# Gated attention and a multiplicative feed-forward network: output tiles of two units paired for seven products, the second unit's gates begun earlier, the weights looked at last

## The chip, the cores and the metric

The kernel runs on one core of one Trainium2 chip. The metric is the device time of one execution in microseconds (us). A profile shows one execution as the hardware profiler recorded it; its "span" leaves out what lies before the first and after the last recorded instruction. TensorE is called PE below, VectorE DVE, ScalarE ACT, GpSimd POOL; SP is the engine that issues the transfers.

## What is computed

Two blocks follow each other. The first is a linear attention with a complex gate per position and channel; the second is a feed-forward network without a nonlinearity except one product.

```python
# q, k, v, a_re, a_im: (4 batches, 8 heads, 768 positions, 48 channels), float32
mag = sqrt(a_re*a_re + a_im*a_im)
scale = minimum(mag, 0.999) / (mag + 1e-06)
for t in range(768):                       # S is a complex 48x48 state per head
    S = (a_re[t] + 1j*a_im[t]) * scale[t] * S + outer(k[t], v[t])
    y[t] = q[t] @ real(S)
x = y with heads side by side              # (3072 tokens, 384)
h = (x @ w1) * (x @ w2) @ w3               # w1, w2: 384x1024, w3: 1024x1024
out = h @ w_out                            # w_out: 1024x384
```

The weights arrive as float64 and are rounded to float32 on the chip; q, k, v and the gates are float32.

## The kernel before

**Units.** The work is cut into 8 units: batch u // 2, half u % 2, 384 positions (TT) in 3 chunks or token tiles of 128. For each unit there are four kinds of work.

- `gates(u)` (L531 to L644) is a generator; each `yield` ends a step. It computes, on ACT and DVE in turn, the running product and angle of the gates: Ln, Exp (L550, L551), a product (L554), its square (L559), Ln (L563), then L567 to L570, the minimum and the scans (L574 to L577), Ln and Exp again, the factors on k and q (L585 to L589), the arc tangent, a scan of angles (L600), its reduction (L607, L608), sines (L611 to L613), four products (L616 to L620). At the end `move` (L627 to L630) issues transfers that regroup k and q by head into the tiles KL and QL, and then the gates, k, q and v of the next unit are loaded (L642, L643). All transfers are issued on the one SP queue.
- The attention of a unit is a list of pieces (`pieces`, L972): `turn` (transposes on PE into tile tp, a copy by ACT into KT, L655), `state` (kv on PE, a sum T on DVE, L710), `scores` (sc on PE, a masked copy by DVE into A, L667), `outputs` (y on PE, a copy by ACT into xT, L694).
- `ffn_ab(u, j)` for j = 0 to 7 (L716): two products m of 384 columns on PE, one copied by ACT (L728), one multiplied by it on DVE into the tile ab (L729).
- The output, ab times w3o, where w3o = w3 @ w_out was made at the start. For units 1 to 7, tiles 0 and 1 of a unit form a pair: the 256x1024 by 1024x384 product is cut into 2x2 blocks and done with 7 block products instead of 8 (Strassen's scheme with 15 sums): `out_sums` makes 4 sums S of blocks of ab (L749), `out_weights` made the sums T of blocks of w3o once (L740), `product` (L762) does 4 steps of 128 rows for a 128x192 block p and adds it into place on DVE (L756). Tile 2 of these units, and all three tiles of unit 0, go through `ffn_out` (L794): 8 matmuls of 384 columns, a copy by ACT, a store. The first product and the second share a PSUM tile (`bank`), so do the third and fourth, and the fifth and sixth. Float32 matmuls are two instructions each in the records.

**Order.** PE's order is written out by hand (`tc.manual_schedule`, L1009); on the other engines a planner orders the instructions by their place in the program and by the dependencies. `tc.high_priority()` moves instructions ahead, and `add_manual_dep` with ORDER fixes an order without a semaphore. `unit(u, ...)` (L993) goes through pieces(u) with the rest of the feed-forward network of unit u - 1 between them, calls the next step of gates(u + 1) after each, and after each piece one `look`.

**The start.** For each of the 8 rows of blocks f, `row_work` rounds w3 and w_out (`load_weight`, L834: ACT writes the rounded low half, for w3 also the sign; DVE shifts and adds), and `fuse` (L935) multiplies them on PE into w3o, whose accumulators hold all 8 PSUM banks. Between the rows stand two steps each of gates(0). w1 and w2 (`w12_work`) are rounded during the attention of unit 0 and the first ab steps. The gates of unit 1 begin at piece 2 of unit 0 (L1054).

**Looks.** `check_weights` (L866) loads the raw weights again after the start, 36 pieces, and the real gates of units 0 and 1, 6 pieces, and tests them for values outside the range in which the fast rounding holds; `judge` (L946) adds up all tests, and a slow general path follows if one failed. Each look runs on ACT (L885 to L888). They start in unit 2, and `judge` comes before the last ffn.

Of the kernel before, what the change touches and what calls it, by code (L numbers as in the profile page):

```python
# [374 lines left out]
def kernel(  # L375
# [47 lines left out]
    HEAD = 8  # L423
    SPLIT = (0,)
# [7 lines left out]
    MIN_SQ, MAX_SQ = 1.126 ** 2, 2.0 ** 32 - 512  # L432
# [30 lines left out]
    consts = singles.tile([P, 7], FP, name="consts")  # L463
    for i, x in enumerate((1.0, LN_EPS, PI / 2, SMALL, -LARGE, MIN_SQ, -MAX_SQ)):
        nc.vector.memset(consts[:, i:i + 1], x)
    ONE, EPS, QUARTER, LEAST, MOST, TINY, TWO = (consts[:, i:i + 1] for i in range(7))
# [8 lines left out]
    st_wts = singles.tile([P, 80], FP, name="st_wts")  # L475
    nc.vector.memset(st_wts, 0.0)
# [11 lines left out]
    def load_gates(u):  # L488
        g = g_t.setdefault(u, {})
        for n, src in (("re", art), ("im", ait)):  # L490
            g[n] = one.tile([P, KD, TT], FP, tag=n, name=n)
            load_rows(g[n], src, u)
# [6 lines left out]
    def load_qkv(u):  # L499
# [5 lines left out]
        load_rows(g["q"], qt, u)  # L505

# [3 lines left out]
        g["vr"] = vr  # L510
# [14 lines left out]
    def chain(ins):  # L525
# [3 lines left out]
        chained[:] = [ins]  # L529

    def gates(u, split):  # L531
# [17 lines left out]
        for s in parts:  # L549
            act(out=A[:, s], in_=re[:, s], func=AF.Ln)  # L550
            act(out=r[:, s], in_=A[:, s], func=AF.Exp, scale=-1.0)  # L551
        yield
# [13 lines left out]
        for s in parts:  # L566
            stt(out=A[:, s], in0=Z[:, s], scalar=0.5, in1=A[:, s], op0=OP.mult, op1=OP.add)  # L567
# [5 lines left out]
        for s in parts:  # L573
            ts(out=A[:, s], in0=A[:, s], scalar1=0.999, scalar2=None, op0=OP.min)  # L574
# [17 lines left out]
        spread_v(u)  # L592
# [16 lines left out]
        yield  # L609
        for s in parts:  # L610
            act(out=re[:, s], in_=Z[:, s], func=AF.Abs)  # L611
            act(out=re[:, s], in_=re[:, s], func=AF.Sin, scale=-1.0, bias=QUARTER)
            act(out=Z[:, s], in_=Z[:, s], func=AF.Sin)  # L613
        yield
        if not split:
            tt(out=r, in0=k, in1=re, op=OP.mult)  # L616
            tt(out=k, in0=k, in1=Z, op=OP.mult)
            yield
            tt(out=A, in0=q, in1=re, op=OP.mult)
# [7 lines left out]
        def move(dst, src, s):  # L627
            for x in range(2):
                for f in range(KD)[s]:
                    nc.sync.dma_start(out=dst[x * KD + f::2 * KD], in_=src[x][:, f])  # L630

        for s in [slice(f, f + 1) for f in range(KD)] if split else parts:
            if split:
                tt(out=r[:, s], in0=k[:, s], in1=re[:, s], op=OP.mult)
                tt(out=k[:, s], in0=k[:, s], in1=Z[:, s], op=OP.mult)
            move(KL, (R, K2), s)
            if split:
                tt(out=A[:, s], in0=q[:, s], in1=re[:, s], op=OP.mult)
# [19 lines left out]
    def scores(u, c, x):  # L658
# [7 lines left out]
        with tc.high_priority():  # L666
            nc.vector.copy_predicated(out=A[:, x * n:(x + 1) * n], data=sc,  # L667
                                      mask=causal.rearrange("p (h t) -> p h t", h=1).to_broadcast([P, n, C]))
# [27 lines left out]
    def state(u, c):  # L696
# [9 lines left out]
        with tc.high_priority():  # L706
            if T is None:
                nc.scalar.copy(out=Tn, in_=kv)
            else:
                nc.vector.tensor_tensor(out=Tn, in0=kv, in1=T, op=OP.add)  # L710
# [412 lines left out]
```

## Time and profile before

| what | us |
|---|---|
| median of 9 executions | 574.75 (574.01 to 576.45) |
| the profiled execution | 574.61 |
| its span | 572.7 |
| first matmul of the rounding (`fuse`, L940) | 7.18 |
| first transpose of unit 0 (L653) | 58.43 |
| first score of unit 0 (L665) | 69.05 |
| first matmul of ffn_ab of unit 0 (L723) | 83.16 |
| last add of an output (L756) begins | 566.69 |

The mean clock granted to PE is 0.991 of full speed. Read it so: up to 83.16 us PE waits for rounding, gates and transfers; from there it hardly stops until 566.7, and the rest of the span is the last store and the test of the flag. Units follow each other about every 62 us (the last products of unit 1's, 2's and 3's output end at 209.90, 271.17 and 333.86). Matmul records overlap, since they are pipelined: a mean duration in a group is longer than the time from one start to the next, which the chain of waits gives.

### The profile page before, as it was taken

The page shows a single profiled execution, that of the slowest core. Times are in us where ns is not written, and L with a number is a line of the kernel's source. Part 1 is how long each engine was busy: PE and PEld are TensorE (multiplying, and loading weights), DVE is VectorE, ACT ScalarE, POOL GpSimd, SP SyncE. Part 2 cuts the span into 40 slices and gives each one's busy share as a digit, 9 for nine tenths or more (in the row PEclk, how much of TensorE's full clock was granted, in tenths as well). Part 3 has the DMA queues.
Part 4 walks back from the last instruction along what each step waited for, and adds up shares of the span by engine and source line. Part 5 has one row for each costly group of instructions (what it writes and reads, how often), then busy time and mean ns, then how long its engine had stood idle before and what let it go on. Part 6 is the DMA issues. An engine that isn't in the chain of part 4 may idle for free.

```text
span 572.7 us, 9280 instructions
## 1 busy us (share of the span) xinstructions
PE 545.4 (95%) x3682; PEld 387.2 (68%) x3682; DVE 335.4 (59%) x507; ACT 347.1 (61%) x569; POOL 3.5 (1%) x9
## 2 busy tenths in 40 slices
PE   4779999999999999999999999999999999999995
PEld 2345775578556985688567976697568966796564
DVE  6898479946852577356752787255743696332121
ACT  6998668537572798558963899279964645101100
POOL 2000000000000000000000000000000000000000
PEclk9899999999999999999999999999999999999998
DMA  8994997393273356954593527844483103300001
GB/s 278 357 378 134 246 340 219 111 232 87 86 160 87 112 150 188 213 172 150 186 211 116 151 74 223 211 144 148 132 196 108 30 27 105 75 2 30 0 1 47
DMA packets 46340, 84.74 MB, mean 148 GB/s; under 512 B 4688, under 2 KB 36176, under 8 KB 45392
## 3 DMA queue, kind: packets, MB, share of 16 engines
q1 hardware_dynamic: 46288, 84.06, 51.7%
q8 instruction: 31, 0.51, 0.4%
q14 instruction: 21, 0.17, 0.1%
HBM read 60.42 MB, written 4.72 MB: 114 GB/s over the span
## 4 chain that ended last, share of the span: by engine, by line
PE 69%; DVE 10%; ACT 10%; DMA 6%; issue 3%; SPq 1%; ACTq 0%; DVEq 0%
PE m L723 38%; PE p L768 10%; PE o L802 7%; PE sc L665 4%; PE kv L703 4%; PE y L692 4%; ACT gZ L544 2%; DMA re<-in_a_re_dram 2%; PE tp L653 2%; ACT gR L544 2%; DMA QL<-gA 1%; DVE gZ L600 1%; DMA look<-in_w_dram 1%; PE f L940 1%; ACT gA L544 1%
## 5 line engine op out<-in xcount | busy, mean ns | idle before, releaser
L723 PE MATMUL m<-xT,w1s 128*128 128x384 f32 x384 | 135.3, 489 | 1.4 <-ACT xT L694 0.8
L723 PE MATMUL m<-xT,w2s 128*128 128x384 f32 x384 | 134.3, 486 | 0.0
L723 PEld LDWEIGHTS m<-xT,w2s 128*128 128x128 f32 x384 | 73.0, 190 | 50.9
L723 PEld LDWEIGHTS m<-xT,w1s 128*128 128x128 f32 x384 | 71.0, 190 | 47.4 <-ACT xT L694 2.0
L729 DVE TENSOR_TENSOR ab<-m,a 128x384 f32<-128x384 f32 x64 | 35.3, 553 | 84.2 <-PE m L723 74.3
L940 PE MATMUL f<-wo_s,w3s 128*128 128x384 f32 x128 | 49.2, 543 | 15.2 <-DVE wo_s L854 15.2
L728 ACT COPY a<-m 128x384 f32<-128x384 f32 x64 | 30.2, 473 | 48.9 <-PE m L723 47.8
L802 PE MATMUL o<-w3o,ab 128*128 128x384 f32 x160 | 54.0, 487 | 0.0
L655 ACT COPY KT<-tp 128x384 f32<-128x384 f32 x40 | 33.5, 849 | 29.2 <-PE tp L653 29.1
L940 PEld LDWEIGHTS f<-wo_s,w3s 128*128 128x128 f32 x128 | 26.7, 214 | 35.1 <-DVE wo_s L854 17.0
L665 PE MATMUL sc<-QL,KL 96*128 96x128 f32 x384 | 47.2, 276 | 1.0 <-issue 0.7
L665 PEld LDWEIGHTS sc<-QL,KL 96*128 96x128 f32 x384 | 45.7, 192 | 2.1 <-issue 0.8
L667 DVE COPY_PREDICATED A<-causal,sc 128x512 f32<-128x512 int32 x48 | 34.4, 740 | 14.5 <-PE sc L665 13.8
L710 DVE TENSOR_TENSOR T<-kv,T 96x512 f32<-96x512 f32 x16 | 11.0, 687 | 54.0 <-PE kv L703 54.0
L802 PEld LDWEIGHTS o<-w3o,ab 128*128 128x128 f32 x160 | 29.6, 190 | 18.7 <-issue 0.4
L692 PE MATMUL y<-A,V 128*32 128x128 f32 x768 | 39.3, 275 | 0.0
L692 PEld LDWEIGHTS y<-A,V 128*32 128x32 f32 x768 | 32.9, 109 | 3.4 <-issue 1.3
L692 PE MATMUL y<-QL,T 96*32 96x128 f32 x640 | 34.6, 272 | 0.0
L768 PE MATMUL p<-To,So 128*128 128x192 f32 x168 | 31.6, 335 | 0.3 <-DVE U L756 0.3
L703 PEld LDWEIGHTS kv<-V,KT 128*96 128x96 f32 x320 | 29.6, 165 | 2.9 <-issue 1.3
L692 PEld LDWEIGHTS y<-QL,T 96*32 96x32 f32 x640 | 31.3, 110 | 0.0
L703 PE MATMUL kv<-V,KT 128*96 128x64 f32 x320 | 30.0, 247 | 1.3 <-ACT KT L655 1.3
(113 smaller groups left out, 742.8 us busy)
## 6 DMA issues: line engine op xcount, KB each, us to landing
look<-in_w_dram SPq DMA_DIRECT2D x28, 512.0 KB, 3.9
raw<-in_w_dram SPq DMA_DIRECT2D x7, 1024.0 KB, 11.1
raw<-in_w_dram SPq DMA_DIRECT2D x8, 768.0 KB, 8.0
KL<-gR SPq DMA_DIRECT2D x24, 192.5 KB, 3.4
KL<-k SPq DMA_DIRECT2D x24, 192.5 KB, 4.0
re<-in_a_re_dram SPq DMA_DIRECT2D x24, 192.0 KB, 5.3
im<-in_a_im_dram SPq DMA_DIRECT2D x24, 192.0 KB, 3.2
k<-in_k_dram SPq DMA_DIRECT2D x24, 192.0 KB, 4.2
```

The lines of the kernel that those rows point to most:

```text
L544: chain(nc.scalar.activation(**kw))
L655: nc.scalar.copy(out=KT_t[u, c][:, :, :, x].rearrange("p h d f -> p f d h"), in_=tp.rearrange("p f (d h) -> p f d h", h=H))
L665: nc.tensor.matmul(out=sc[:, j], lhsT=KL[:, x * n + j, w], rhs=QL[:, x * n + j, w], start=True, stop=True)
L667: nc.vector.copy_predicated(out=A[:, x * n:(x + 1) * n], data=sc, mask=causal.rearrange("p (h t) -> p h t", h=1).to_broadcast([P, n, C]))
L692: nc.tensor.matmul(out=o, lhsT=a, rhs=b, start=s0, stop=s1)
L703: nc.tensor.matmul(out=kv[:, hd], lhsT=KT[:, hd].rearrange("p d x f -> p (d x f)"), rhs=V[:, hd], start=True, stop=True)
L723: nc.tensor.matmul(out=m, lhsT=w[:, j * P // WB, f, j * P % WB:j * P % WB + P], rhs=xT_t[u][:, f], start=(f == 0), stop=(f == KD - 1))
L728: copied[:] = [nc.scalar.copy(out=a, in_=got[0])]
L729: nc.vector.tensor_tensor(out=ab_t[u][:, j], in0=got[1], in1=a, op=OP.mult)
L768: nc.tensor.matmul(out=m[p], lhsT=a[:, f], rhs=b[:, f], start=(f == 0), stop=(f == KH - 1))
L802: nc.tensor.matmul(out=m, lhsT=ab_t[u][:, f, t * P:(t + 1) * P], rhs=w3o[:, f], start=(f == 0), stop=(f == KF - 1))
L940: nc.tensor.matmul(out=sums[j], lhsT=w3_t[f][:, j * P:(j + 1) * P], rhs=w3_t["wo"][:, f], start=(f == 0), stop=(f == KF - 1))
```

## The change

1. **Output.** `ffn_out` is gone. A pair is a list of two (unit, tile): in even units tiles 1 and 2, in odd units tiles 0 and 1, and then tile 0 of the even unit with tile 2 of the odd one. So there are 12 pairs with 7 products each, and no output tile of 8 matmuls. The tile ab holds 512 columns, of which the odd unit overwrites the last 384. The order of the products is the same, 1, 2, 4, 6, 7, 5, 3, with other PSUM tiles: (1, 4), (2, 6), (7, 3), (5). The first product is copied into a tile U1 and not into the output. Stores come after the next unit's moves.
2. **The second unit's gates.** Five steps of gates(1) are taken at piece 0 of unit 0 (none at pieces 1 to 5, one from piece 6 on); the sum T of unit 0's chunk 1 waits in order for the last sum of step 5; the minimum of step 6 comes after the last masked copy seen so far. The gates of unit 1 are loaded inside gates(0), before its moves; the cosine of unit 0 goes to another tile so that `re` is free for it.
3. **Weights looked at last.** A look is now three instructions on DVE (sign bit off, clamp, compare and count). Units 2 to 5 take a look at every fourth piece, units 6 and 7 at every piece, and the rest goes between the ab steps of the last unit; `judge` follows that unit's first product.
4. **The start.** Row 1 is loaded and rounded in two halves, its sign on DVE; the steps of gates(0) are dealt 3, 2, 2, 2, 1, 1; v of unit 0 is loaded after row 3 and spread at the end; w1 and w2 are rounded with the sign on ACT, after the moves.

```diff
+    def load_v(u):
...
+        if u:
+            load_v(u)
...
             act(out=r[:, s], in_=A[:, s], func=AF.Exp, scale=-1.0)
+            if u == 1:
+                tc.add_manual_dep(chained[-1].ins, fused[-1].ins.name, ORDER, reason="unit 0 first")
...
-            stt(out=A[:, s], in0=Z[:, s], scalar=0.5, in1=A[:, s], op0=OP.mult, op1=OP.add)
+            begun[:] = [stt(out=A[:, s], in0=Z[:, s], scalar=0.5, in1=A[:, s], op0=OP.mult, op1=OP.add)]
...
-            ts(out=A[:, s], in0=A[:, s], scalar1=0.999, scalar2=None, op0=OP.min)
+            least = ts(out=A[:, s], in0=A[:, s], scalar1=0.999, scalar2=None, op0=OP.min)
+            if u == 1:
+                tc.add_manual_dep(least.ins, masked[-1].ins.name, ORDER, reason="scores first")
...
+        cos = A if u == 0 else re
+        if u == 0:
+            load_gates(1)
...
-                nc.vector.tensor_tensor(out=Tn, in0=kv, in1=T, op=OP.add)
+                add = nc.vector.tensor_tensor(out=Tn, in0=kv, in1=T, op=OP.add)
+                if (u, c) == (0, 1):
+                    tc.add_manual_dep(add.ins, begun[-1].ins.name, ORDER, reason="begun")
...
-            ab_t[u] = one.tile([P, KF, TT], FP, tag="ab", name="ab")
+            if u % 2 == 0:
+                ab_t["two"] = one.tile([P, KF, TT + P], FP, tag="ab", name="ab")
+            ab_t[u] = ab_t["two"][:, :, u % 2 * P:u % 2 * P + TT]
...
-    def out_sums(u):
-        S = s_t["S"] = late.tile([P, 4, KH, P], FP, tag="S", name="So")
-        A = [[ab_t[u][:, i * KH:(i + 1) * KH, t * P:(t + 1) * P] for i in range(2)] for t in range(2)]
+    def out_sums(tiles):
+        S = late.tile([P, 4, KH, P], FP, tag="S", name="So")
+        A = [[ab_t[u][:, i * KH:(i + 1) * KH, t * P:(t + 1) * P] for i in range(2)] for u, t in tiles]
...
-        def product(n, i, p):
+            store = nc.sync.dma_start(out=out[r0:r0 + P, :], in_=o[i])
+            after = moved.get(max(u for u, _ in tiles) + 1)
+            if after:
+                tc.add_manual_dep(store.ins, after.ins.name, ORDER, reason="moves first")
+
+        def product(p, bank, i):
+            if p == 1:
+                out_sums(tiles)
             if i == 0:
-                m["bank"] = ps_m.tile([P, 2, DH], FP, tag="mm", name="p")
-            m[p] = m["bank"][:, i]
+                m[bank] = ps_m.tile([P, 2, DH], FP, tag="mm", name="p")
+            m[p] = m[bank][:, i]
...
-                    nc.scalar.copy(out=o[0][:, 0:DH], in_=m[1])
+                    nc.scalar.copy(out=U[1], in_=m[1])
...
-        return [lambda n=n, p=p: product(n, n % 2, p) for n, p in enumerate((1, 2, 4, 6, 7, 5, 3))]
-
-    def ffn_out(u, t, parts=1):
...
+        return [lambda p=p, b=b, i=i: product(p, b, i) for p, b, i in (
+            (1, "a", 0), (2, "b", 0), (4, "a", 1), (6, "b", 1), (7, "c", 0), (5, "d", 0), (3, "c", 1))]
...
+        elif not sign_act:
+            nc.vector.tensor_scalar(out=low, in0=hi, scalar1=-0x80000000, scalar2=0x3F800000, op0=OP.bitwise_and,
+                                    op1=OP.bitwise_or)
...
-                    follow([nc.scalar.activation(out=hi, in_=hi, func=AF.Square, scale=2.0 ** 15)])
-                    nc.scalar.activation(out=lo, in_=hi, func=AF.Relu, scale=-1.0, bias=TINY, accum_out=st_wts[:, n:n + 1])
-                    if w is w3t:
-                        nc.scalar.activation(out=hi, in_=hi, func=AF.Relu, bias=TWO, accum_out=st_wts[:, n + 40:n + 41])
+                    follow([nc.vector.tensor_scalar(out=hi.bitcast(I32), in0=hi.bitcast(I32), scalar1=0x7FFFFFFF,
+                                                    scalar2=None, op0=OP.bitwise_and)])
+                    nc.vector.tensor_scalar(out=lo, in0=hi, scalar1=MIN_HI, scalar2=MAX_HI if w is not wo else 3.0e38, op0=OP.max,
+                                            op1=OP.min)
+                    nc.vector.scalar_tensor_tensor(out=lo, in0=hi, scalar=1.0, in1=lo, op0=OP.mult, op1=OP.is_equal,
+                                                   accum_out=st_wts[:, n:n + 1])
...
-            load_weight((w1s, w2s)[i][:, n], got[n][i])
+            load_weight((w1s, w2s)[i][:, n], got[n][i], True)
...
-    def ffn(u, parts=1):
-        if u == 0:
-            return [lambda j=j: ffn_ab(u, j) for j in range(KF)] + [p for t in range(UC) for p in ffn_out(u, t, parts)]
-        got, last = out_pair(u), ffn_out(u, UC - 1, parts)
-        if parts == 2:
-            got.insert(5, last[1])
-        return [lambda j=j: ffn_ab(u, j) for j in range(KF)] + [lambda: (out_sums(u), last[0]())] + got
+    def ffn(u):
+        got = [lambda j=j: ffn_ab(u, j) for j in range(KF)] + out_pair([(u, 1 - u % 2), (u, 2 - u % 2)])
+        return got + (out_pair([(u - 1, 0), (u, UC - 1)]) if u % 2 else [])
...
-            next(look, None)
+            if u > NU - 3 or i % 4 == 0:
+                next(look, None)
...
-        row_load(1)
+        row_load(1, 2)
...
-            for _ in range(2):
+            for _ in range((3, 2, 2, 2, 1, 1)[f]):
                 next(steps, None)
         work = w12_work()
+        for _ in steps:
+            pass
+        spread_v(0)
         for f in work[:2]:
             f()
-        for _ in steps:
-            pass
...
-        load_gates(1)
...
-            if i >= 2:
+            for _ in range(5 if i == 0 else i >= 6):
                 next(steps)
...
-        for _ in look:
-            pass
-        judge()
-        for f in ffn(NU - 1, 2):
+        for i, f in enumerate(ffn(NU - 1)):
             f()
+            for _ in range(2):
+                next(look, None)
+            if i == KF:
+                for _ in look:
+                    pass
+                judge()
```

## The prediction

> **What bounds the kernel now.** I read the busy times and the clock first, then PE's idle time by stage, then the chain of waits, then the groups.
>
> ```profile
> PE 545.4 (95%) x3682; PEld 387.2 (68%) x3682; DVE 335.4 (59%) x507; ACT 347.1 (61%) x569; POOL 3.5 (1%) x9
> PE   4779999999999999999999999999999999999995
> PEclk9899999999999999999999999999999999999998
> ```
>
> PE is busy all through, at full clock, except in the first three slices of 14.3 us. So the time is PE's start plus PE's work plus few gaps. The start, from the timeline of PE (start, length, count, idle time before and its releaser):
>
> ```profile
> 7.18 8.21 PE L940 MATMUL f<-wo_s,w3s 128*128 128x384 f32 x16 [7.18 <-DVE wo_s L854]
> 19.66 17.43 PE L940 MATMUL f<-wo_s,w3s 128*128 128x384 f32 x48 [4.26 <-DVE wo_s L854]
> 40.33 14.75 PE L940 MATMUL f<-wo_s,w3s 128*128 128x384 f32 x40 [3.25 <-DVE wo_s L854]
> 55.56 2.85 PE L940 MATMUL f<-wo_s,w3s 128*128 128x384 f32 x8 [0.47 <-DVE wo_s L854]
> ```
>
> PE waits there for DVE's rounding (rows 1 and 4). Later gaps, from the table of stretches (stretch, then PE's busy time out of its length):
>
> ```profile
> 125.00:130.00 5.00, 4.35 (x41) 4.12 (x40) 2.26 (x4) 1.17 (x2) 0.00 (x0) 1.00 1.08 279
> 155.00:160.00 5.00, 4.41 (x14) 2.39 (x13) 2.25 (x4) 3.58 (x5) 0.00 (x0) 1.00 0.40 118
> 400.00:420.00 20.00, 18.61 (x60) 10.84 (x59) 15.78 (x19) 18.98 (x36) 0.00 (x0) 1.00 0.46 140
> ```
>
> That is 0.65 + 0.59 + 1.39 = 2.6 us idle; the last one is a transpose that waited 1.4 us for gR (L616), behind looks on ACT. The rates come from the chain (start, us, what), in unit 2:
>
> ```profile
> 181.11 5.16 PE o L802 x16
> 186.60 1.33 PE kv L703 x16
> 187.93 1.37 PE p L768 x8
> 189.69 1.57 PE p L768 x8
> 191.26 1.33 PE kv L703 x16
> 192.59 1.84 PE sc L665 x16
> 194.43 1.30 PE p L768 x8
> ```
>
> A tile by `ffn_out` takes 5.16 us, a block product 1.30 to 1.57. Between the first two products PE stands still:
>
> ```profile
> PEld p L768 <- ACT ot L776: 1.7, 4, 0.7
> PE p L768 <- ACT ot L776: 0.4, 1, 0.4
> ```
>
> The second product shares the first one's PSUM tile and waits until ACT has copied it.
>
> **1. Output.** Before: 10 tiles by `ffn_out` = 10 x 5.16 = 51.6 us, and 7 pairs. After: 12 pairs. The five new pairs are 35 products; at the rate of the last two in the last unit (x16 in 2.61 us, 1.305 each) they take 45.7: **-5.9 us**. At the mean of a pair inside unit 2 (1.37 + 1.57 + 1.30 + 1.50 + 1.50 + 2.80 = 10.04 for 7) it is 50.2, or -1.4; that is the upper end, -6.3 (1.293 each, half of o) the lower. I take -5.9 and charge +1.0 by itself for the slower products after kv and y (five groups more, 0.2 each). The pairs' sums are DVE work: 4 x 0.69 + 7 x 0.35 = 5.2 us a pair, 26 us in all, beside 335 us busy of 573; the first sum is needed only by the fourth product, 3.9 us after the first. ACT loses ten copies of 0.47.
>
> **2. PSUM tiles.** Products 1 and 2 no longer share a tile. The waits shown are 2.1 us, those for the adds (DVE U) 0.8: -2.9 at best, 0 at worst if other copies hold ACT. I take **-2.5**. In the last unit the count matmul takes one of the four PSUM tiles, so that product 5 there waits for the adds after product 7, two of 0.36: +0.8, in the new waits below.
>
> On weight loads: a product has one load of 128 columns for 192 columns of matmul, an o instruction one for 384. 5.16/16 = 322 ns an instruction and 1.30/8 = 162: just half, so that the load is hidden in both. The Trainium skill ("TensorE: Matmul & The Clock Gate", section "The mechanism") says that a load overlaps a matmul in flight only if it goes to other rows of the array, and its section "LDWEIGHTS (loading the stationary operand)" puts 128 columns at 128/1.2 = 107 ns; by that, as an estimate, the change's 120 more loads would cost 12.8 us and the output would become slower by 7. The trace of before decides against it.
>
> **3. Start.** Row 1 in two halves: DVE and ACT reach it at about 13.7 and 14.3 as now. ACT's low half of 512 (about 0.73, between 0.49 for 256 and 1.34 for 1024) ends at 15.0, DVE's add ends near 15.9, wo_s near 17.3: PE starts row 1 at 17.3 instead of 19.66. Row 4 is still DVE's: it falls earlier by the wait of 1.65 (at 17.91), by a scan, a small copy and a reduction that now come after it (0.94 + 0.17 + 0.55), and later by the sign halves (about 1.1): 40.3 becomes 38.2. Rows 5 to 7 keep DVE's pace, so the first transpose comes at 55.8 to 56.4 instead of 58.43. The moves of unit 0 are no longer held behind the transfers of w1 and w2 (SP issued the first at 50.68; its gR, L634, was there at 42.3), so KL and QL land before PE gets to the scores, at 66.4 instead of 69.05.
>
> Then DVE is late. Before the first xT is complete it now has: the last T sum and its product with rho 2 x 0.69, six masked copies 6 x 0.74, two blocks of w1 and w2 (4 shifts of 0.55, 4 adds of 0.95), the minimum 0.76 and three scans 2.65; with 0.09 of overlap each, some 14 us from 66.3, and one Ln (1.16) stands ahead of the third xT copy (0.46) on ACT. So m starts at about 82.3 instead of 83.16: **-0.9**. If DVE kept up, PE's own work would put it at 80.1 (-3.1); if the w1 and w2 transfers, now behind the moves, came late (8.0 us to landing each, four in a row), at 86 (+3). The five early steps pay off later: gR of unit 1 is ready near 104 instead of 113.6, so unit 1's scores and unit 2's gates (first Ln now 128.83) have about 6 us to spare.
>
> One row on the clock: after the wait of 4.26 us the granted clock is 0.69 in 20 to 25 us, after 3.25 it is 0.66 in 40 to 45, after 0.47 it is 1.00. The Trainium skill (same page, section "What's actually happening") makes that an idle window of some 3.4 us; by it the shortened wait at row 1 would keep the clock and give about 1.5 us. None of it is in my sum, since DVE sets row 4.
>
> **4. Gaps.** ACT loses the looks: 28 x (0.69 + 0.77 + 0.19), 16 x 0.96 and 8 x 1.4, near 73 us. That removes what delayed gR in 400 to 420. Of the 2.6 us idle I take **-2.0** (0 to -2.6).
>
> **5. What is late next.** A look on DVE is about 0.42 + 0.42 + 0.69 + 0.08 = 1.6 us (rows L844, L852, L749 at 384 to 768 columns; the test itself is not in the trace: between 0.35 x 3 and 1.0 x 3). 36 of them put 58 us on DVE: 335 + 26 + 58 = 419 of some 565, 74%. They stand in unit 6 (11), unit 7 (10) and the last ab steps. Gates(7), on DVE from 447.8 to 483.0 now, have eight looks between them: 13 us, of which DVE's idle 7.4 us there takes part; gR was 5 us ahead of its transpose and unit 6 gets 4 us longer. In odd units a single product (1.3) instead of o (5.16) stands between the last transpose and the last kv, against a copy of 0.85 on ACT: up to 0.5 each in four units. With the 0.8 from above: **+1.5** (0 to +6).
>
> **Sum.** -5.9 + 1.0 - 2.5 - 0.9 - 2.0 + 1.5 = -8.8. The profiled execution took 574.61 (span 572.7 and 1.9 around it), 0.14 below the median of 574.75; 574.61 - 8.8 = **565.8 us**.
>
> **Rivals.** *It does more* (0.14): DVE keeps up at the start (-3.1), products run at half of o without transitions (-6.3), all gaps and tile waits go (-2.6, -2.9): -14.9, 559.7. For it: PE's own order has nothing else to wait for. Against: DVE's full windows up to 85 us.
>
> *The saving turns into waits in the odd units and in unit 6* (0.13): the forecast's -8.8, and then +4 for gates(7), which the looks make late by what its 5 us ahead and the 4 us more of unit 6 do not cover, +1 for copies that hold the products as the shared tile did, +0.9 for a start that gains nothing: -2.9, 571.7.
>
> *The change does not do what it says* (0.05): the early steps end behind the same DVE work and the pairs cost what the tiles cost: 573.6 to 575.9.
>
> *Slower* (0.08): the looks stop PE. Each look's first instruction waits on DVE for its transfer, and ab's product (L729) is queued behind it, so that PE runs out of PSUM tiles (four, two ab steps, 7.7 us). With two buffers a look takes (landing + 1.6)/2; the landing is 3.9 now: 2.75 us. Ten looks stand between the first and the seventh ab of the last unit, 23.2 us; they need 27.5, and 4.3 late is less than 7.7. It decides from (landing + 1.6)/2 x 10 > 30.9, a landing above 4.6 us. At 6 us, near moves and stores, the last stage loses 7 us and units 6 and 7 as much again: 565.8 + 14 = 580.
>
> **Numbers.** The forecast has 0.60, with a range of its own of 562 to 569.5. Faster by over 0.2% (below 573.6; about what a measurement of this kernel can tell) 0.60 + 0.14 + 0.13 = 0.87; same 0.05; slower 0.08. The range of 8 in 10 holds the forecast, the waits and half of the first rival: 560 to 572.5.
>
> **What would show it.** Right: no group o; p x672 at 326 ns; no wait of p for ACT; first L940 matmul after the first row at about 17, m first at 80 to 83; DVE near 75%, ACT near 50%; idle of PE after 85 us below 3 us. Wrong: m first after 85 us; L729 waiting for looks on DVE in the last unit; a transpose of unit 7 waiting for gR; p's mean interval above 1.43 us a product.

## The result and the profile after

The changed kernel takes 578.87 us (median of 10 executions, 576.26 to 580.12), the kernel before 574.42 (median of 31). The ratio is 1.0073, with a 95% interval from 1.0060 to 1.0086: slower by 0.7%, where 565.8 was forecast and 572.5 was the upper end. The profiled execution of the changed kernel took 580.12, the slowest of its ten; its span is 578.3.

The busy times, PE's slices and the clock, from the page of the changed kernel:

```profile
PE 542.7 (94%) x3802; PEld 402.4 (70%) x3802; DVE 401.7 (69%) x703; ACT 293.6 (51%) x432; POOL 3.5 (1%) x9
PE   4788889999999999999999999999999899999996
PEclk9889998999999999999999999999999999999998
```

PE has 2.7 us less to do than before, ACT 54 less, DVE 66 more. But PE's slices, 14.5 us each, stand at 8 instead of 9 in the fourth to sixth (43 to 87 us) and again in the thirty-second (448 to 463), and the clock has an 8 instead of a 9 in the third and the seventh. Between 85 and 500 us PE is idle for 415 - 405.3 = 9.7 us; before it was 3.5.

The start, from the timeline of PE (start, length, idle time before and its releaser in brackets):

```profile
18.65 7.12 PE L970 MATMUL f<-wo_s,w3s 128*128 128x384 f32 x16 [3.25 <-DVE wo_s L879]
26.77 10.59 PE L970 MATMUL f<-wo_s,w3s 128*128 128x384 f32 x32 [1.00 <-DVE wo_s L879]
39.60 14.78 PE L970 MATMUL f<-wo_s,w3s 128*128 128x384 f32 x40 [2.24 <-DVE wo_s L879]
56.07 2.85 PE L970 MATMUL f<-wo_s,w3s 128*128 128x384 f32 x8 [1.69 <-DVE wo_s L879]
```

Row 1 comes 1.0 us earlier than before, row 4 0.7, but two waits have come up (1.00, and 1.69 instead of 0.47), and the last eight begin at 56.07, half a microsecond later than before. This execution was late from its first matmul on (7.86 us). In the eleven other profiles with this start the first matmul came at 7.02 to 7.46, row 1 at 16.85 to 18.24 and row 4 at 37.80 to 39.18.

Five of PE's later waits, from the same view:

```profile
85.93 2.93 PE L748 MATMUL m<-xT,w1s 128*128 128x384 f32 x6 [2.38 <-ACT xT L714]
144.58 2.20 PE L748 MATMUL m<-xT,w1s 128*128 128x384 f32 x6 [1.43 <-ACT xT L714]
...
451.02 1.57 PE L803 MATMUL p<-To,ab 128*128 128x192 f32 x8 [1.60 <-ACT U L812]
...
469.83 2.20 PE L748 MATMUL m<-xT,w1s 128*128 128x384 f32 x6 [0.85 <-DVE ot L785]
552.03 2.20 PE L748 MATMUL m<-xT,w2s 128*128 128x384 f32 x6 [0.97 <-DVE ab L754]
```

The first six m take 2.93 us at 85.93 and 2.20 in the other places: after the wait the clock is 0.73 in 85 to 90 us and 0.93 in 90 to 95. That loss belongs to this execution: the stage of unit 1, 58.7 us in the table below, takes 56.9 to 57.0 in six other profiles with the same wait (2.32 to 2.44 us) and a clock of 1.00.

The stages show where the time came from. A stage runs from the first m after one unit's attention to the next such m; "counted" is what the prediction's rates make of it (a product 1.305, a tile by `ffn_out` 5.16: 7 products for 3 tiles in unit 1, 7 products for a tile in even units and at the end, a tile less in odd units). The last column is the fastest kernel of the experiments, e17.

| stage | before | counted | after | e17 |
|---|---|---|---|---|
| up to the first m | 83.2 | | 85.9 | 81.6 |
| unit 1 | 63.1 | -6.3 | 58.7 (-4.4) | 57.5 (-5.6) |
| unit 2 | 63.4 | +4.0 | 67.9 (+4.5) | 66.6 (+3.2) |
| unit 3 | 61.4 | -5.2 | 56.8 (-4.6) | 55.8 (-5.6) |
| unit 4 | 62.6 | +4.0 | 69.0 (+6.4) | 66.5 (+3.9) |
| unit 5 | 61.5 | -5.2 | 56.9 (-4.6) | 55.8 (-5.7) |
| unit 6 | 64.1 | +4.0 | 69.7 (+5.6) | 67.0 (+2.9) |
| unit 7 | 61.2 | -5.2 | 56.9 (-4.3) | 56.0 (-5.2) |
| the last, to the last add | 46.2 | +4.0 | 50.9 (+4.7) | 49.5 (+3.3) |

In the changed kernel every stage is dearer than counted: unit 4 by 2.4 and unit 6 by 1.6; the start is 2.8 later than in the kernel before. The next sections find three causes. The largest is on the queue of SP, in the even units. There the real gates of the next unit are loaded, and they open its chain of gates. In unit 6 of the kernel before, from the timeline of SP:

```profile
424.94 2.15 SPq L485 DMA_DIRECT2D re<-in_a_re_dram  x3
```

and the first Ln of gates(7), from its timeline of ACT, which waits for nothing:

```profile
439.87 1.17 ACT L544 ACTIVATE gA<-re 128x1152 f32<-128x1152 f32 x1
```

In the changed kernel the two stores of the pair that ends in the same unit stand ahead of that load, and SP waits with them for the pair's last sums:

```profile
418.40 2.08 SPq L650 DMA_DIRECT2D QL<-q  x3
440.59 1.90 SPq L790 DMA_DIRECT2D out_dram<-ot  x2
442.58 1.88 SPq L489 DMA_DIRECT2D re<-in_a_re_dram  x3
```

SP's own waits name what the stores wait for, the sums into the output tile (us in total, times, longest; the whole execution):

```profile
SPq L790 <- DVE ot L785: 124.8, 14, 21.0
```

The first Ln of gates(7), from ACT's timeline of the changed kernel, waits for the load, and the copy of a product that PE needs comes after it:

```profile
448.36 1.16 ACT L556 ACTIVATE gA<-re 128x1152 f32<-128x1152 f32 x1 [9.91 <-DMA re<-in_a_re_dram]
...
450.67 0.30 ACT L812 COPY U<-p 128x192 f32<-128x192 f32 x1
```

SP idles from 420.5 to 440.6 and the Ln comes at 448.4 instead of 439.9, although the stage begins at 395.2 in both kernels. The copies of U and xT that PE needs stand behind gates on ACT: that is the 1.60 at 451.02. Units 2 and 4 show the same wait of the Ln, 8.39 and 8.29 us.

### The profile page after: what moved, and what is told of

It reads as the page before. It is cut to its first block, busy times and chain, and to the rows that moved or that the text cites. A ratio compares the mean times of both kernels' runs of the same rounds, so it can differ in the third digit from the quotient of the medians.

```text
span 578.3 us, 9581 instructions
## 1 busy us (share of the span) xinstructions
PE 542.7 (94%) x3802; PEld 402.4 (70%) x3802; DVE 401.7 (69%) x703; ACT 293.6 (51%) x432; POOL 3.5 (1%) x9
## 4 chain that ended last, share of the span: by engine, by line
PE 61%; DVE 16%; DMA 10%; ACT 7%; issue 4%; SPq 2%; ACTq 0%; DVEq 0%
PE m L748 34%; PE p L803 14%; DMA look<-in_w_dram 5%; PE kv L723 4%; PE sc L685 3%; PE tp L673 2%; ACT gZ L556 2%; PE y L712 2%; PE f L970 2%; DMA look<-in_w_out_dram 2%; DVE gA L592 2%; DMA re<-in_a_re_dram 1%; SPq L489 1%; DMA im<-in_a_im_dram 1%; DVE A L687 1%
## 5 line engine op out<-in xcount | busy, mean ns | idle before, releaser
L748 PE MATMUL m<-xT,w2s 128*128 128x384 f32 x384 | 135.9, 490 | 2.1 <-DVE ab L754 2.1
L748 PEld LDWEIGHTS m<-xT,w2s 128*128 128x128 f32 x384 | 72.9, 192 | 55.8 <-DVE ab L754 6.5
L754 DVE TENSOR_TENSOR ab<-m,a 128x384 f32<-128x384 f32 x64 | 35.1, 551 | 48.1 <-PE m L748 44.9
L970 PEld LDWEIGHTS f<-wo_s,w3s 128*128 128x128 f32 x128 | 26.2, 211 | 36.1 <-DVE wo_s L879 18.8
L785 DVE TENSOR_TENSOR U<-p,U 128x192 f32<-128x192 f32 x36 | 12.7, 353 | 33.1 <-PE p L803 33.1
L803 PE MATMUL p<-To,So 128*128 128x192 f32 x192 | 35.5, 332 | 0.0
L803 PE MATMUL p<-w3o,So 128*128 128x192 f32 x192 | 34.6, 331 | 0.9 <-DVE U L785 0.9
L803 PE MATMUL p<-w3o,ab 128*128 128x192 f32 x192 | 35.2, 330 | 0.0
L556 ACT ACTIVATE re<-gZ 128x1152 int32<-128x1152 f32 (+2 forms) x17 | 17.8, 1047 | 32.7 <-DVE gZ L617 24.1
L803 PEld LDWEIGHTS p<-w3o,So 128*128 128x128 f32 x192 | 30.9, 190 | 2.9 <-DVE U L785 1.5
L803 PEld LDWEIGHTS p<-To,So 128*128 128x128 f32 x192 | 31.0, 190 | 1.8 <-issue 1.8
```

The costliest lines, as they stand in the source:

```text
L556: chain(nc.scalar.activation(**kw))
L748: nc.tensor.matmul(out=m, lhsT=w[:, j * P // WB, f, j * P % WB:j * P % WB + P], rhs=xT_t[u][:, f], start=(f == 0), stop=(f == KD - 1))
L754: copied[:] = [nc.vector.tensor_tensor(out=ab_t[u][:, j], in0=got[1], in1=a, op=OP.mult)]
L785: nc.vector.tensor_tensor(out=out, in0=x, in1=y, op=OP.add)
L803: nc.tensor.matmul(out=m[p], lhsT=a[:, f], rhs=b[:, f], start=(f == 0), stop=(f == KH - 1))
L970: nc.tensor.matmul(out=sums[j], lhsT=w3_t[f][:, j * P:(j + 1) * P], rhs=w3_t["wo"][:, f], start=(f == 0), stop=(f == KF - 1))
```

## The experiments

All medians were compared with the kernel before, run on the same chip beside them (574.3 to 575.1). Ratios have 95% intervals. A difference between two experiments is that of their medians.

### Looks: none, and on ACT (e1, e2)

```diff
-        look = check_weights(...)
+        look = iter(())
```

> The changed kernel without any look: the tests of the raw weights and of the real gates of units 0 and 1 are left out, with their transfers; the judgement stays. Theory (a look's first instruction waits on DVE for its transfer, and the ab products and sums of outputs stand behind it, in the stages of units 4, 6 and 7): the gaps of PE after 85 us, 9.7 us in the profile of the changed kernel, shrink by 5 to 7, and the time goes from 578.9 to 572 to 574. Rival (all of the loss comes from the start and from products that are slower than half a tile): the time stays within 1.5 of 578.9, and DVE's 58 us of looks lie in its idle time.

Measured: 577.06, ratio 1.0049 (1.0030 to 1.0068). That is outside the 572 to 574 expected: leaving the looks out gives 1.8 us here, and the intervals with looks (1.0060 to 1.0086) and without overlap. The end of unit 6 still loses 2.75 us to xT, and 1.43 are still lost at 141: the gaps were not the looks' alone.

e2 puts the tests of the kernel before back: on ACT, one after each piece, `judge` ahead of the last ffn.

> The changed kernel with the looks of the kernel before: on ACT, one a piece from unit 2 on, judged before the last feed-forward stage. Theory of the looks on DVE: 573 to 575, that is nearly all that leaving them out gives, since ACT has room; the last stage, 50.9 us from its first m to its last product now, falls to 48.5 or less. Rival (looks cost the same on either engine, because their transfers hold up the moves and loads of the next unit): within 1.5 of 578.9.

Measured: 579.28, ratio 1.0097 (1.0063 to 1.0132): no gain at all. PE waits for xT five times, 8.0 us in all. Its last stage has no wait; it is the even units 2 and 4 above all that got worse (70.1 and 70.4 us, 67.9 and 69.0 in the changed kernel). My reading is that ACT has gates that come late and now the looks too; e14 below, the same kernel with the stores moved, bears it out with 66.6 and 66.5. The theory that the looks were the cause by themselves fell with these two.

### Gates(1) as before (e3)

```diff
-            for _ in range(5 if i == 0 else i >= 6):
+            if i >= 2:
                 next(steps)
```

and the orders "unit 0 first", "scores first" and "begun" are gone.

> The changed kernel with one step of gates(1) after each piece from piece 2 on, as before, and without the three orders that went with the five early steps. Theory (five early steps put DVE work and one Ln ahead of the state sums and of the third xT copy, so that m starts at 85.9 instead of 83.2, and PE's wait costs its clock as well): m starts at 83 to 84, the first ab stage ends near 114.5 instead of 118.7, and the time falls by 3.5 to 4.5, to about 574.7. Rival (the w1 and w2 blocks and the moves set the start, not the gates): m still at 85 to 86, time within 1 of 578.9. A second rival: the start is regained, but gates(1) and gates(2) are late by as much, and the wait of 1.43 at 143 us grows: -1 to -2.

Measured: 600.51, ratio 1.0439 (1.0425 to 1.0453), a miss by 26 us. PE's timeline shows it at once:

```profile
87.59 3.78 PE L681 MATMUL sc<-QL,KL 96*128 96x128 f32 x16 [13.00 <-DVE A L683]
```

With the orders I had taken away what keeps gates(1) behind the masked copies of unit 0: the gates of unit 1 are loaded early in this kernel, and so the planner put minimum, scans and three more steps of gates(1) on DVE from 72.1 to 86.3, ahead of the first masked copy (86.8). The orders are a working part of the change. That the loss comes from them and not from the later steps is read from this timeline; the two were not undone one at a time. Of the start e3 told nothing; e8 and e10 do.

### Pairs alone, with the stores in three places (e4, e7, e6)

Part 1 is put into the kernel before, with the smaller buffers that the first expectation names: same start, gates, and looks on ACT. Only the store differs between the three.

```diff
 e4             nc.sync.dma_start(out=out[r0:r0 + P, :], in_=o[i])
 e7  -          nc.sync.dma_start(out=out[r0:r0 + P, :], in_=o[i])
     +          store = nc.sync.dma_start(out=out[r0:r0 + P, :], in_=o[i])
     +          ...
     +          tc.add_manual_dep(store.ins, after.ins.name, ORDER, reason="moves first")
 e6  -          nc.sync.dma_start(out=out[r0:r0 + P, :], in_=o[i])
     +          nc.gpsimd.dma_start(out=out[r0:r0 + P, :], in_=o[i])
```

> The kernel before with part 1 of the change alone: 12 pairs with the new PSUM tiles and U1 in place of pairs and whole tiles, with the ab tile of 512 columns; to make room for it the low words of the rounding have one buffer of 4 KB and one of 3 KB, and the weights' sums T are three blocks, as in the changed kernel. Start, gates, looks and the order of stores are those of before. Theory (products cost half of a tile, as counted): -5.9 + 1.0 and up to -2 for the PSUM tiles: 567.5 to 570. Rival (the products' load rows, kv transitions and DVE sums eat it): 573 to 575.5, no gain.

> Pairs alone, stores on SP's queue but ordered after the next unit's moves, as in the changed kernel. Theory of the store that blocks the next load: no wait for QL, but the first Ln of the gates waits 8 to 10 us for the real gates in units 2, 4 and 6: 2 to 5 above the run with stores on POOL, so 570 to 575. Rival (moves first cures all): equal to the run with stores on POOL within 1.

> The run with pairs alone, which took 597.4, with its stores issued by POOL on a queue of its own. Theory (its loss is three waits of PE for QL, 20.9 us, behind stores on SP's queue, and the clock after them; the products themselves cost half a tile as counted): 567 to 570, against 574.9 for the kernel before. Rival (with the queue free the products, their sums on DVE and the copies still eat the gain): 573 to 576.

| | median | ratio (interval) |
|---|---|---|
| e4, stores where the planner puts them | 597.42 | 1.0393 (1.0374 to 1.0412) |
| e7, after the moves | 581.66 | 1.0125 (1.0103 to 1.0148) |
| e6, issued by POOL | 571.06 | 0.9941 (0.9924 to 0.9958) |

The same products cost 26 us more or less by where a store stands on a queue. All three lie above their forecasts, e4 by 27 us, e7 by 7 and e6 by 1. In e4 SP holds the moves of QL: it issues moves of KL up to 166.5 us and then nothing until a store. Two rows of its timeline, and then one of PE's:

```profile
188.08 0.34 SPq L765 DMA_DIRECT2D out_dram<-ot  x1
188.52 0.56 SPq L630 DMA_DIRECT2D QL<-gA  x1
```

```profile
196.96 3.33 PE L665 MATMUL sc<-QL,KL 96*128 96x128 f32 x14 [6.94 <-DMA QL<-q]
```

Three such waits of PE make 20.9 us. "Moves first" removes them, and the stores then hold the next thing on the queue: in e7 the first Ln of the gates waits 7.7, 8.9 and 9.4 us in units 2, 4 and 6. With the stores on POOL no Ln after unit 1's waits, and the pairs gain 3.2 us. The theory of the changed kernel is confirmed for the queue; the gain is smaller than I expected. Unit 1 fell by 2.3 us only (60.8), not by the 6.3 counted: it now ends in a wait of 2.07 for xT at 144.2, and unit 2 begins with a loss of clock in this execution.

### The changed kernel, stores on POOL (e5), and the control (e11)

```diff
-            store = nc.sync.dma_start(out=out[r0:r0 + P, :], in_=o[i])
-            after = moved.get(max(u for u, _ in tiles) + 1)
-            if after:
-                tc.add_manual_dep(store.ins, after.ins.name, ORDER, reason="moves first")
+            nc.gpsimd.dma_start(out=out[r0:r0 + P, :], in_=o[i])
```

> The changed kernel with one difference: the stores of the outputs are issued by POOL on a queue of its own, so that none stands on SP's queue between the moves and the load of the next unit's real gates. Theory (the store blocks: in units 2, 4 and 6 the first Ln of the next gates waits 8.3 to 9.9 us for that load, the chain of gates then runs into the last xT copy, and PE waits for it): these waits of ACT go, PE's waits for xT after 85 us (1.4 + 2.4 there, 4 to 5 without looks) shrink to below 1, and the time falls by 3 to 6, to 573 to 576. Rival (the looks on DVE alone make the gaps): within 1.5 of 578.9.

Measured: 572.53, ratio 0.9976 (0.9954 to 0.9998), 6.3 us below the changed kernel by the medians, a little more than forecast, and 5.6 by the ratios, whose intervals lie apart. PE's idle time between 85 and 500 us falls from 9.7 to 4.0. The Ln of gates(7) no longer waits. It comes 43.1 us after the first m of unit 6's stage (386.5), where it was 53.2 in the changed kernel (395.2):

```profile
429.59 1.16 ACT L556 ACTIVATE gA<-re 128x1152 f32<-128x1152 f32 x1
```

> The kernel before with the stores issued by POOL on a queue of its own, nothing else: a control. In it no gate waits for a store (the only Ln that waits for its load is that of unit 2, 5.8 us, and its load stands behind no store). Theory: the same, 574.3 within 0.8. Rival (stores on SP cost the kernel before something too, or POOL's issue costs by itself): more than 1 away.

Measured: 576.79, ratio 1.0028 (1.0017 to 1.0040). So POOL's queue is no gain in itself: with the order of before it costs 1.7 us, as the rival said. What that is made of I did not find. Nothing here suggests that the gain of e5 comes from faster or parallel transfers.

### The stores on SP, behind the next gates' load (e13)

```diff
+            after = gated.get(max(u for u, _ in tiles) + 2)
+            if after:
+                tc.add_manual_dep(store.ins, after.ins.name, ORDER, reason="gates first")
```

where `gated[u]` is the last transfer of the real gates of unit u.

> The changed kernel, stores still on SP's queue, with one more order: a pair's stores come after the load of the next unit's real gates as well as after the moves. Only three places on the queue change (units 2, 4 and 6: load ahead of two stores). Theory (the store that waits for its sums holds that load, hence the chain of gates, hence xT): as with the stores on POOL or better, since POOL's issue cost the kernel before 1.6: 570.5 to 573, from 578.9. Rival (the gain on POOL came from something else, such as shorter queues or earlier free tiles): above 576.

Measured: 575.56, ratio 1.0014 (1.0003 to 1.0026): 3.3 us gained, about half of what POOL gave, and between what theory and rival had said. The Ln comes on time (309.8 in unit 4), but now k, q and the look stand behind the stores. SP in unit 4:

```profile
291.14 1.88 SPq L489 DMA_DIRECT2D re<-in_a_re_dram  x3
312.16 0.82 SPq L795 DMA_DIRECT2D out_dram<-ot  x2
313.09 3.24 SPq L489 DMA_DIRECT2D k<-in_k_dram  x3
316.38 1.88 SPq L489 DMA_DIRECT2D q<-in_q_dram  x3
318.30 8.35 SPq L918 DMA_DIRECT2D look<-in_w_dram  x3
```

And DVE in the same stretch:

```profile
324.65 0.44 DVE L920 TENSOR_SCALAR look<-look 128x512 int32<-128x512 int32 x1 [3.90 <-DMA look<-in_w_dram]
```

A look that waits 3.9 us for its transfer holds DVE; the gates, two masked copies and the sums of a pair follow it, and PE waits 2.29 for a sum at 334.5 and 0.95 for xT. So the place on the queue is a cause by itself, since here no queue was added; and each load that stays behind the stores passes the wait on.

### What looks cost with the queue free (e9, e14)

Both are e5 with another choice for the looks: none in e9; those of before, on ACT, one after each piece from unit 2 on, in e14.

> The changed kernel with the stores on POOL's queue and without any look (the tests of the raw weights and of the real gates of units 0 and 1 are left out). It prices the looks on DVE where the gates are on time. Theory (a look holds up DVE's queue by its transfer and its 1.6 us): the wait of 0.93 for ab in the last unit and the 1.95 for xT at the end of unit 6 with the clock lost after it go: 2 to 4 below the 572.5 of the run with looks. Rival (the stores were the whole cause, and looks cost nothing with the queue free): within 1 of 572.5.

> The changed kernel with the stores on POOL's queue and the looks of before on ACT, one a piece from unit 2. It stood at 572.5 with looks on DVE and at 568.1 without looks. Theory (looks on DVE hold up sums and scans, on ACT they fit): 568.5 to 570.5. Rival (ACT in even units is as full of waits as DVE, the looks cost the same there): 572 to 574.

Measured: e9 568.08, ratio 0.9886 (0.9871 to 0.9902); e14 568.12, ratio 0.9883 (0.9868 to 0.9898). On DVE the looks cost 4.4 us, on ACT nothing that can be told from leaving them out. The profiles of e5 and e9 differ in the last three stages, where most looks stand: 68.7 us against 66.5 in unit 6, 57.6 against 55.8 in unit 7, 50.9 against 49.7 in the last. At the end of unit 6 PE waits 1.95 for xT in e5, and in unit 7 the clock is 0.74 in 457 to 462 us; e9 has neither. From unit 1 to unit 5 the two agree within 0.1 us a stage.

Looks and stores are not independent. With the stores on SP after the moves, leaving the looks out gave 1.8 (e1) and putting them on ACT nothing (e2). Read the other way, taking the stores off SP gave 6.3 us with looks on DVE (e5), 9.0 without looks (e1 to e9) and 11.2 with looks on ACT (e2 to e14).

### The start (e8, e10)

Parts 2 and 4 are undone; pairs and looks on DVE stay. In e8 the stores are on SP after the moves, as in the changed kernel, in e10 on POOL.

> The changed kernel with the start, gates(1) and rounding of before (parts 2 and 4 undone; pairs, moves first and the looks on DVE stay). Theory (early gates put DVE and ACT work ahead of the state sums and of xT): first m at 83.2 to 83.6, the first ab stage ends at 114.5, and the time is 2.5 to 4.5 below the changed kernel, 574.5 to 576.5. Rival (the early gates give it back later, through gates(2) and the wait of 1.43 at 143 us): within 1 of 578.9, with a longer wait before the m of unit 1.

> The changed kernel with the start and gates(1) of before, and the stores on POOL's queue: parts 2 and 4 undone with the queue free. First theory (the early gates cost the 1.3 to 4 us by which the first ab stage ends later): 569 to 571, below the 572.5 of the run with the new start. Second theory (formed after the run with the old start, 580.6 against 578.9: the early gates give more back at the end of unit 1, where m starts at 141.8 instead of 143.5 to 144.5): 573.5 to 575.5.

Measured: e8 580.62, ratio 1.0102 (1.0082 to 1.0123), against 1.0073 with the new start; e10 574.87, ratio 1.0001 (0.9989 to 1.0014), against 0.9976. My first theory of the start, that it costs 2.5 to 4.5 us, is wrong: the new start gains 1.7 and 2.3 by the medians. The gain itself is small against the noise: in both pairs the intervals overlap a little. With the old one m of unit 0 comes earlier (83.6 in e8, 84.5 in e10, against 84.8 in e5), but m of unit 1 later: 143.5 and 144.4 against 141.8 in e5. The early gates pay in unit 1, whose stage takes 59.9 us in e8 and e10 and 56.9 in e5; at its end xT of the old start waits 2.07.

### xT ahead of the Ln (e12)

e5, and on ACT the first Ln after the scans of gates(1), and the three small copies that wait for the same scans, are ordered after the third xT copy of unit 0. For that the steps of gates(1) behind it are dealt later: none from piece 7 on, and two with each of the first three ab steps.

```diff
             act(out=r[:, s], in_=A[:, s], func=AF.Ln)
+            if u == 1:
+                tc.add_manual_dep(chained[-1].ins, placed[-1].ins.name, ORDER, reason="xT first")
...
+            last = nc.scalar.copy(out=X, in_=A[:, :, TT - 1])
+            if u == 1:
+                tc.add_manual_dep(last.ins, placed[-1].ins.name, ORDER, reason="xT first")
...
-            for _ in range(5 if i == 0 else i >= 6):
+            for _ in range(5 if i == 0 else i == 6):
...
-            if i < 6:
+            for _ in range(2 if i < 3 else i < 6):
```

The reason for it is in ACT's timeline of the changed kernel:

```profile
84.35 1.17 ACT L556 ACTIVATE gR<-gA 128x1152 f32<-128x1152 f32 x1 [3.50 <-DVE gA L592]
85.42 0.46 ACT L714 COPY xT<-y 128x384 f32<-128x384 f32 x1
```

ACT stands 3.5 us before an Ln whose scans DVE has not finished, and the copy that PE waits for is next.

> The changed kernel with the stores on POOL's queue, and with the first Ln after the scans of gates(1), and the three small copies that wait for the same scans, ordered after the third xT copy of unit 0 on ACT. Theory (xT stands behind an Ln that waits for DVE's scans): PE's wait of 2.3 to 2.4 us at 84 falls below 0.7, the clock stays at 1.00 there, m starts at 82.3 to 83, and the time is 1 to 3 below 572.5. Rival (w2s, which DVE finishes at 82 to 83, sets the first m anyway, or gates(1) are late by as much): within 0.7 of 572.5.

Measured: 569.45, ratio 0.9898 (0.9884 to 0.9913), 3.1 us below e5. PE's wait at 84 is gone; the first m follows the last f directly, at 83.5 in this execution.

### All three (e15, e16, e17)

e15 and e17 mend all three causes, e15 with the stores on SP as in e13, e17 with them on POOL. e16 is e15 with the looks on DVE.

> All three causes mended, work complete: stores on SP behind the load of the next gates, the Ln after the scans of gates(1) ordered behind the third xT copy, looks on ACT as before. If the three causes are independent: 578.9 - 6.4 - 3.0 - 3 = 565 to 568, below both kernels. Rival (they overlap, as the looks on ACT gained nothing by themselves): 569 to 571.

Measured: 570.85, ratio 0.9933 (0.9911 to 0.9955), as the rival said. In units 2 and 4 a sum and xT are still 1.0 to 1.2 late: k, q and looks stand behind the stores on SP, as in e13.

> As the run before in this list, but the looks stay on DVE and are spread, one a piece from unit 2 on, and judged before the last feed-forward stage. It parts the engine of the looks from their place. If the place is the cause (eleven in unit 6, ten at the last ab steps): 565.5 to 568.5, no wait for ab in the last unit. If the engine is (DVE's queue waits for each transfer): 569 to 572, with the waits now in units 2 to 5.

Measured: 578.32, ratio 1.0074 (1.0051 to 1.0097), 7.5 us above e15, which differs in the looks themselves alone (on ACT, at the same places), and above the 569 to 572 expected for the engine. So with the stores on SP it is the engine and not the late place. The spread place was no help on DVE: e13, with the late looks and without the order on xT, took 575.56. The largest of PE's waits after the start:

```profile
PE tp L682 <- DVE gR L645: 7.0, 3, 4.2
```

The looks now delay the gates themselves, and transposes wait for gR.

e17 is e12 with the looks of before, on ACT.

> All three causes mended, work complete: stores on POOL's queue, the first Ln after the scans of gates(1) ordered behind the third xT copy, looks on ACT as before. The run with the first and third took 568.1; the order alone gave 3.0 where looks were on DVE. If they add up: 565 to 566.5, about what was forecast for the change (565.8). Rival (what xT gains is lost again at the end of unit 1, where PE waits 1.4 for the last xT): 567.5 to 568.5.

Measured: 565.99, ratio 0.9862 (0.9839 to 0.9885): 1.4% faster than the kernel before, with all the work done. These waits of PE follow the rounding:

```profile
PE kv L725 <- ACT KT L677: 1.4, 2, 0.9
PE m L750 <- ACT xT L716: 1.4, 1, 1.4
PE sc L687 <- DVE A L689: 1.2, 4, 0.5
PE m L750 <- DVE ab L756: 0.4, 1, 0.4
PE tp L675 <- DVE gR L638: 0.2, 1, 0.2
```

The profiles of e14 and e17 agree within 0.1 us in each of the seven stages from unit 2 on; they differ in the first m, 85.28 against 81.60, of which unit 1 gives back 0.5.

From the changed kernel to e17 the medians go 578.87, 572.53 (stores, 6.3), 568.12 (looks, 4.4), 565.99 (xT, 2.1): together 12.9, and 13.1 lay between forecast and result. The split holds for this order only, as the 6.3, 9.0 and 11.2 above show. And that e17 ends within 0.2 of the forecast is in part luck: it keeps the looks on ACT, which the forecast took off, and its terms differ from the forecast's, as the next section shows.

## Why the prediction was wrong

**Step 1, output: right.** Seven stages of e17, from unit 2 to unit 7 and the last, together take 417.2 us, before 420.4: 3.2 less. Counted are 3 x -5.2 + 4 x 4.0 = +0.4; the other 3.6 are about what step 2 (-2.5) and the two gaps of step 4 that lie there (0.59 and 1.39) were to give. Unit 1 fell by 5.6 of 6.3. The products did not become slower: p has a mean of 330 to 332 ns an instruction (326 were named), and no tile by `ffn_out` is left. The 120 loads of weights more cost nothing that could be seen, against the estimate from the Trainium skill that the prediction weighed.

**Step 2, PSUM tiles: right in kind.** The four waits of the second product for ACT's copy are gone. The one wait of p for ACT in the changed kernel (1.60) is for the same copy, which now stood behind the late Ln on ACT; e17 has none. The 0.8 for the count matmul did not show.

**Step 3, start: the sum was nearly right, the way was not.** Forecast -0.9 at the first m; measured +2.8 in the profiled execution (first m between 84.2 and 85.3 in the other profiles with this start and no order on xT), and then -1.7 to -2.3 in the time, because the early gates make the stage of unit 1 3.0 us shorter (59.9 in e10, 56.9 in e5). Of the points on the way, row 1 came at 18.65 (17.3 forecast), row 4 at 39.60 (38.2), the latest of all profiles with this start; e17 had 16.85 and 37.80. The last rows waited for DVE in all of them (1.6 to 2.9 us), and the scores came at 69.8, in e17 at 68.0, not at 66.4. I had seen "one Ln ahead of the third xT copy" and charged its 1.16 us; its real price is the wait of that Ln for the scans, 3.5 us of ACT, and 2.1 to 3.1 us of time (e12, e17). The bound "+3" of that step (m at 86) had the right number by luck: it was priced for late transfers of w1 and w2.

**Step 4, gaps: wrong.** -2.0 was taken, and they grew by 6.2 (3.5 to 9.7). The cover went as the looks left ACT, but the Ln of three units then waited behind a store: with the stores on POOL (e5) 4.0 are left.

**Step 5, what is late next: here the forecast failed.** It asked which instructions stand behind a look on DVE, and which behind copies on ACT, but for the last sentence of part 1 of the change, that stores come after the next unit's moves, it had no price. The term missing is three waits of SP for the sums of a pair (18.8, 21.1 and 20.1 us in units 2, 4 and 6), with the loads for the next gates behind them: 6.3 us (e5; e4, e7, e6 and e13 for the mechanism), and more where the looks are on ACT or left out. The looks on DVE were in the term, which was +1.5 with ends 0 and 6; 0.8 of it was the count matmul's, so at most 0.7 was for looks, and they cost 4.4 (e9).

**The rivals.** The one on the other side named the looks, DVE's queue and a price of 14 from a landing (from a look's issue to its arrival) above 4.6 us. Its 580 lies near the 578.87 measured, but by luck. It had a true part: looks did wait for their transfers, 12.5 us on DVE for those of in_w, and they cost 4.4, in the stages that it named (units 6, 7 and the last). But the landing is 4.1, below its 4.6, and in the last unit, where it was worked out, PE waited 0.97 once (552.03), not 7; the larger loss is the stores', of which it says nothing. "The saving turns into waits in odd units and in unit 6" had unit 6 right as a place, though the Ln there waited for the load behind the stores and not for looks, and the odd units wrong: units 3, 5 and 7 fell by 4.3 to 4.6 of 5.2.

**The signs named.** Of the wrong signs "m first after 85 us" came true (85.93); the product into ab (L754, L729 before) stood behind looks in the last unit but cost PE only 0.97, and no transpose of unit 7 waited for gR. Of the right ones, no group o, 672 products p, and DVE 69% and ACT 51% (75% and 50% named) came; m at 80 to 83, no wait of p for ACT, and PE idle below 3 us after 85 (9.7 up to 500) did not.

On queues, the Trainium skill ("Trainium Kernel Development and Optimization", section "Key Constraints") says that issuing transfers from several engines only saves the sequencer's issue time. The two stores take SP 0.82 us to issue in units 2 and 4, off PE's path; by the rule POOL's queue would have given next to nothing, and e11, where it gave nothing, agrees with that. In e5 it gave 6.3 us, because in these traces SP issued nothing behind a store while the store waited, for 18.8 to 21.1 us.

## What to carry to other kernels

When a result is finished later than before, follow its store: on a queue in order, what stands behind a store that waits is late by as much, and an order that puts the store after one transfer only passes the wait on to the next one. Price an instruction on a shared engine not by its length but by the wait that it brings with it, and look whether something short that the bounding engine needs is queued behind it. Undoing a part together with the orders written for it tests something else than the part.

## What the runs showed of the hardware

The same wait before the first m of unit 1 (2.07 to 2.08 us, after xT) costs the clock or does not. Stretch from 145 to 150 us (PE busy, PEld, DVE, ACT, POOL; granted clock third from the end), of e6 and then of e7:

```profile
145.00:150.00 5.00, 5.00 (x12) 2.78 (x11) 3.88 (x4) 3.28 (x7) 0.00 (x0) 0.69 0.39 121
```

```profile
145.00:150.00 5.00, 5.00 (x17) 2.93 (x16) 3.88 (x5) 3.00 (x7) 0.00 (x0) 1.00 0.39 121
```

e6 begins 12 matmuls in that stretch, e7 17: some 1.5 us lost or not. In e10 the clock was 0.66, in e8 0.82, in e4 1.00. Waits of 2.32 to 2.44 before the first m of unit 0 gave 0.73 in the changed kernel and 1.00 in e1, e2, e5, e9, e13 and e14. Waits of 1.42 to 1.44 before the first m of unit 1 left the six m at 2.20 us in all eleven profiles that have them. The Trainium skill ("TensorE: Matmul & The Clock Gate", section "What's actually happening") has the clock halved after an idle window of about 3.4 us; here 2.1 us were enough in some executions. At row 1 of the start, too, a shorter wait did not always keep the clock, which the prediction's reading of that section made of it: it was 0.80 in 15 to 20 us after 2.33 us in e1 and 0.74 after 2.61 in e17, but 1.00 after 2.36 in e5.
